# FFT-style convolution on one core: second pixels held behind the third weight chunk, and weight, transform and plane operations of the two-tile phase put in another order

## The chip, the core and the metric

The kernel runs on one core of a Trainium2 chip. The core has five engines that run side by side and meet only through semaphores. TensorE (PE) multiplies matrices; PEld is its load of the stationary operand. VectorE (DVE) and ScalarE (ACT) do elementwise work and move results out of PSUM, the accumulator memory of eight banks. GpSimd (POOL) does slow elementwise work. SyncE (SP) issues transfers, which sixteen DMA engines carry out. The metric is the device time of one execution in microseconds (us); lower is better. Of the kernel before, three runs are shown: 271.89, 271.96 and 272.75 us, median 271.96.

## The reference

The input is one image of 224 x 224 pixels with 96 channels; the weights are 7 x 7 taps from 96 to 96 channels, all bf16. The reference multiplies spectra, which is a circular convolution:

```
Xf = rfft2(x, axes=(1, 2))                     # 1 x 224 x 113 x 96
Wf = rfft2(pad(w to 224 x 224), axes=(0, 1))
Yf = einsum('bhwi,hwio->bhwo', Xf, Wf)
y  = irfft2(Yf, s=(224, 224), axes=(1, 2)).astype(bfloat16)
```

## The kernel before, in words

The image's width is cut into seven tiles of 32 pixel columns (index t). In the height direction the kernel uses blocks of 28 output rows and a short transform of them into 17 frequency slots (index s, 0 to 16); slots 0 and 16 are real, the others have three parts (real, imaginary and the difference of the two). Along the width the seven taps stay a direct convolution, in a form for two output pixels at a time that shares products.

The work of a tile has these steps.

1. **Transform** (`f_jobs`, `a_jobs`): matmuls of pixels with the transform matrix `Fm`; the result is moved ("evicted") from a PSUM bank into `xf`. For the first three tiles it is done in three parts of slots (`SH2`: 0-7, 8-12, 13-16). `jg` is the half of the image's rows; each half has its own pixel buffer.
2. **Planes** (`jit`): for a group of two or three slots VectorE forms `J` from `xf` in three operations: first four planes of differences of pixels, then one sum of parts, and third two planes made from the first four. Three `J` buffers take turns.
3. **Rounds** (`b_round`): one round is one slot of one tile. TensorE multiplies `xf` and `J` with the transformed weights `WF` into two banks. ScalarE makes a scaled copy (`tt_`), VectorE forms `u` from the first bank (which frees it) and `v` from the second. POOL then adds `v` and `u` into `yf` (`ysum`). Real slots have a single VectorE operation instead.
4. **Way back**: `yf` goes to a scratch array in DRAM, is read again with another layout (`tt`), multiplied with `G` and written out.

The weights are loaded in five chunks of columns (`wcut`), each as two transfers, and transformed on TensorE from `wq` (`prep_jobs`), in six groups of slots (`PGRP`). Group 0 comes before the rounds; the others are paced inside them. A group of the others has 12 matmul jobs and, on VectorE, three differences.

The order is written out by hand. Each engine runs its instructions in program order. `fills` is called twice in a round, as `mid` between the two banks and as `end`; it hands out jobs that `add(a, b, jobs)` has spread evenly over the call numbers a to b - 1. The eviction of a bank goes to VectorE or ScalarE by a running cost count (`evac`). Bank number n + 8 of the sequence waits for the eviction of bank n.

In the two-tile phase the rounds of tile 0 and tile 1 run together, tile 1 four rounds behind (`LAG`). `bursts` says in which round which group of planes is formed; a round's planes stand behind its `v`, and POOL's sum of that round waits for the last of them. Ahead of it lie the loads, set-up work on POOL, VectorE and ScalarE, the transform of tile 0's first half, filler matmuls on `wu` (`warm`) that compute nothing that is used, the transform of weight group 0, and the transform of the second half's first part. The first tile's pixels (`load_x(0, 0)`, `load_x(0, 1)`) are loaded into the tail of `WF`, which a late weight group overwrites; the second tile's loads wait for an eviction.

Of the kernel before, what the change touches and what calls it, by code (L numbers as in the profile page):

```python
# [17 lines left out]
NS = L // 2  # L18
# [14 lines left out]
PGRP = ((0, 2), (2, 5), (5, 8), (8, 11), (11, 14), (14, 17))  # L33
# [6 lines left out]
JGB = ((0, 3), (3, 6), (6, 9), (9, 12), (12, 15), (15, 17))  # L40
LAG = 4
# [3 lines left out]
NP2 = 0  # L45
WARM = 36
NWC = 5
BIAS = 3000.0


# [5 lines left out]
def kernel(  # L56
# [7 lines left out]
    _, H, W, C = x.shape  # L64
# [8 lines left out]
    C2 = C // 2  # L73
    assert NJ == 8
    SYNC = mybir.DependencyInfo(mybir.DependencyClass.Sync, mybir.DependencyReason.DATA)
# [57 lines left out]
    def dma(out_ap, in_ap):  # L133
        return DE.dma_start(out=out_ap, in_=in_ap)
# [18 lines left out]
    wqx = wtmp.tile([128, C - 1 + 127 * C + 1], BF16, name="wq")  # L153
# [20 lines left out]
    def load_x(t, jg):  # L174
        return load_rows(xbuf(t, jg), jg, t * 2 * TW, 2 * TW)

    wsrc = w.rearrange("kh kw i o -> (kh kw) (i o)")
    for jg in range(2):
        load_rows(xh_bufs[jg], jg, W - PAD, PAD)
    load_x(0, 0)  # L180
    wcut = [WC * c // NWC // 128 * 128 for c in range(NWC)] + [WC]
    for c0, c1 in zip(wcut, wcut[1:]):
        for k, n in ((PW - 1, 1), (0, PW - 1)):
            dma(wqx[2 * k:2 * (k + n), c0:c1],
                bass.AP(wsrc.tensor, wsrc.offset + k * C * C + c0, [[C * C, n], [C2, 2], [1, c1 - c0]]))
    load_x(0, 1)

    wu = cpool.tile([128, 128], BF16, name="wu")
    wur = wu[:].unsqueeze(1).to_broadcast([128, 4, 128])
# [2 lines left out]
    def warm(n):  # L192
        pwu = bank()
        for _ in range(n):
            TE.matmul(pwu[:].rearrange("p (a b) -> p a b", a=4), lhsT=wu[:, 0:128], rhs=wur, start=True, stop=True)
# [297 lines left out]
    def b_round(t, s, mid, end, ydve=False, planes=()):  # L493
# [26 lines left out]
        if s in REAL:  # L520
            for part in range(2):
                conv(b0, part * C, 0, part)
            SE.copy(out=tt_[:, 0:2 * C], in_=b0[:, 0:2 * C])
            mid()
            for mi, m in enumerate((2, 1)):
                for part in range(2):
                    conv(b1, (mi * 2 + part) * C, m, part)
            VE.tensor_tensor(out=yv.rearrange("p r m o -> p m r o"),
                             in0=tt_[:, 0:2 * C].rearrange("p (r o) -> p r o", o=C).unsqueeze(1).to_broadcast([128, 2, 2, C]),
                             in1=b1[:, 0:4 * C].rearrange("p (m r o) -> p m r o", m=2, r=2), op=ALU.add)  # L530
            load["a"] += 110 + 0.9 * 192
            load["v"] += 540
            for f in planes:
                f()
            end()
        else:
            v = tv_pool.tile([128, 2, 2, C], F32, name="v")
            if merge:
                conv(b0, 2 * C, 0, 0, both=True)
                conv(b0, 2 * C, 2, 0, add=True)  # L540
                conv(b0, 3 * C, 1, 0, add=True)
                conv(b0, 0, 0, 1)
                conv(b0, C, 0, 2)
                SE.mul(out=tt_[:], in_=b0[:, 0:4 * C], mul=-0.5)
                u, pr = tt_[:, 2 * C:4 * C].rearrange("p (m o) -> p m o", m=2), tt_[:, 0:2 * C]
            else:
                for part in range(3):
                    conv(b0, part * C, 0, part)
                conv(b0, 3 * C, 2, 0)
                conv(b0, 4 * C, 1, 0)  # L550
                u = tv_pool.tile([128, 2, C], F32, name="u")
                SE.mul(out=tt_[:, 0:3 * C], in_=b0[:, 0:3 * C], mul=-0.5)
                pr = tt_[:, C:3 * C]
            if puts:
                puts.pop(0)()
            if not merge:
                VE.scalar_tensor_tensor(out=u[:], in0=b0[:, 3 * C:5 * C].rearrange("p (m o) -> p m o", m=2), scalar=-0.5,
                                        in1=tt_[:, 0:C].unsqueeze(1).to_broadcast([128, 2, C]), op0=ALU.mult, op1=ALU.add)
            mid()
            for mi, m in enumerate((2, 1)):  # L560
                for pi, part in enumerate((1, 2)):
                    conv(b1, (mi * 2 + pi) * C, m, part)
            VE.scalar_tensor_tensor(out=v.rearrange("p m r o -> p m (r o)"),
                                    in0=pr.unsqueeze(1).to_broadcast([128, 2, 2 * C]), scalar=-2.0,
                                    in1=b1[:, 0:4 * C].rearrange("p (m q) -> p m q", m=2), op0=ALU.mult, op1=ALU.add)
            def ysum(eng):
                return eng.tensor_tensor(out=yv.rearrange("p r m o -> p m r o"), in0=v[:],
                                         in1=u.unsqueeze(2).to_broadcast([128, 2, 2, C]), op=ALU.add)
            if ydve:
                ysum(VE)  # L570
            last = None
            for f in planes:
                last = f()
            if not ydve:
                y = ysum(GE)
                if last is not None:
                    tc.add_manual_dep(y.ins, last.ins.name, SYNC, reason="sum after planes")
            load["a"] += 490 if merge else 410
            load["v"] += (560 if ydve else 250 if t < 2 else 0) + (560 if merge else 900)
            end()  # L580
# [119 lines left out]
    fj = [f_jobs(0, p) for p in range(3)]  # L700
    for p in range(3):
        for f in fj[p][0]:
            f()
    for _ in range(3):
        warm(9)
    for f in prep_jobs(0):
        f()
    last = [f() for f in fj[0][1]]
# [29 lines left out]
    def add(a, b, jobs):  # L738
        qs.append([a, b, jobs, len(jobs)])

    for gi in range(1, len(PGRP)):
        add(2 * PGRP[gi - 1][0], 2 * PGRP[gi - 1][1] - 1, prep_jobs(gi))
    for t in range(2):
        scr_tiles[t] = dr_pool.tile([TW, NJ, NS, 4 * C], BF16, name="scr")
    bursts = {}
    for g in range(len(JGB)):
        g0 = JGB[g][0]
        if g:
            bursts[(g0 - 2, 1 if g0 - 2 >= LAG else 0)] = (0, g)
        r1 = LAG + g0 - (3 if g == len(JGB) - 1 else 1)  # L750
        bursts[(r1, 0 if r1 < NS else 1)] = (1, g)
    bursts[(NS + LAG - 2, 1)] = (2, 0)
    nburst = len(bursts)
    for r in range(NS + LAG):
        if r == 0:
            add(0, 4, fj[1][1] + fj[2][1])
        for p in range(3):
            if r == (1, 3, 5)[p]:
                new_xf(1, SH2[p], SH2[p + 1])
                fj = f_jobs(1, p)  # L760
                if p == 2:
                    for jg in range(2):
                        fj[jg][-1] = then_load(fj[jg][-1], 2, jg)
                add(2 * r + 1, 2 * r + (5, 5, 4)[p], fj[0] + fj[1])
        for p in range(3):
            if r == SH2[p + 1] + 1 - (p == 2):
                new_xf(2, SH2[p], SH2[p + 1])
                fj = f_jobs(2, p)
                if p == 2:
                    for jg in range(2):  # L770
                        fj[jg][-1] = then_load(fj[jg][-1], 3, jg)
                add(2 * r, 2 * r + (8, 7, 5)[p], fj[0] + fj[1])
        if r == PGRP[-2][1] + 1:
            assert not any(q[2] for q in qs[:len(PGRP) - 1])
            wtmp_cm.__exit__(None, None, None)
            t_pool = ctx.enter_context(tc.tile_pool(name="tt", bufs=NTT, side="right"))
            t2_pool = ctx.enter_context(tc.tile_pool(name="tt2", bufs=1, side="right"))
            yo_pool = ctx.enter_context(tc.tile_pool(name="yo", bufs=2, side="right"))
            g_pool = ctx.enter_context(tc.tile_pool(name="gp", bufs=1, side="right"))
            GA = g_pool.tile([KA, 4 * B], BF16, name="GA")  # L780
            GB = g_pool.tile([128, 2, 4 * B], BF16, name="GB")
            GE.memset(GA[:], 0.0)
            GE.memset(GB[:], 0.0)
        if r == NS + 3:
            queue_c(0)
        for t in range(2):
            s = r - LAG * t
            if not 0 <= s < NS:
                continue
            now = bursts.pop((r, t), ())  # L790
            now = jit(*now) if now else ()
            both = LAG <= r < NS
            b_round(t, s, fills(qs, 2 * r + (t if both else 0)), fills(qs, 2 * r + (t if both else 1)), False, now)
    assert not bursts and nburst == 2 * len(JGB)
    if NP2:
        ps0_cm.__exit__(None, None, None)
        ps_cms = [tc.tile_pool(name="ps", bufs=NP2, space=bass.MemoryType.PSUM),
# [4 lines left out]
    for t in range(2, NT):  # L802
# [22 lines left out]
        for s in range(NS):  # L825
            now = ()
            if s in plan:
                g = plan[s]
                now = jit(t, g + 1) if g + 1 < len(JGB) else jit(t + 1, 0)
# [34 lines left out]
    for i, (g, q) in enumerate(order):  # L864
# [3 lines left out]
        k = i + 8 - LF  # L868
# [37 lines left out]
```

## Time and profile before

| | |
|---|---|
| median of the runs shown | 271.96 us |
| profiled execution, its own time | 272.2 us |
| its span | 270.5 us |
| TensorE busy | 258.7 us (96%) |
| VectorE busy | 213.9 us (79%) |
| ScalarE busy | 195.6 us (72%) |
| POOL busy | 95.6 us (35%) |
| granted TensorE clock | 1.00 |
| DMA, mean rate | 173 GB/s |
| chain that ended last | 74% TensorE |

The views give times in us from the start of the span. A timeline row has start, duration, engine, source line, operation, output and inputs, and in brackets how long the engine had been idle and what ended that. A duration of a merged row runs from the first start to the last end. All operations go through one recording helper, so that nearly every row has its line, L88; tiles tell the rows apart. A row by stretches has the stretch, its length, and the busy time of PE, PEld, DVE, ACT and POOL with the number of instructions in brackets, then the granted clock, the share of the DMA engines' time and GB/s. DMA rows of SPq show the issue, not the transfer.

### The profile page before, as it was taken

To read this page: it belongs to the slowest core of one execution; us is meant where nothing else is said; L and a number is where in the kernel's file an instruction comes from. 1 tells how busy PE (TensorE), PEld (TensorE's weight loads), DVE (VectorE), ACT (ScalarE), POOL (GpSimd) and SP (SyncE) were. 2 spreads that over 40 slices of the span, in tenths; PEclk is the share of its full clock that TensorE was granted. 3 is DMA by queue.
4 is the path that set the end of the run, shared out by engine and by line. 5 is a ranking of instruction groups with operands and counts; after the bars stand their busy time and mean duration, and the time that the engine had idled before them with its cause. 6 is when DMAs were issued, how large, how long until landed. Compare 5 with 4: busy or idle time off the path is not lost.

```text
span 270.5 us, 12170 instructions
## 1 busy us (share of the span) xinstructions
PE 258.7 (96%) x5149; PEld 237.8 (88%) x5149; DVE 213.9 (79%) x457; ACT 195.6 (72%) x483; POOL 95.6 (35%) x156
## 2 busy tenths in 40 slices
PE   8899998999999999999999999999999999899983
PEld 3679898999999989999999999998998989789862
DVE  5647999898889888779787888787898889778623
ACT  5549997568875657988988889887887865477113
POOL 7781032435536624431422222223222242422100
PEclk9999999999999999999999999999999999999999
DMA  6947010731121498986977477989649834887766
GB/s 168 232 124 200 23 47 2 204 105 49 43 77 63 126 276 157 292 247 177 298 206 217 116 205 244 251 210 349 222 125 163 269 103 147 200 235 203 221 118 202
DMA packets 47014, 46.78 MB, mean 173 GB/s; under 512 B 35286, under 2 KB 37986, under 8 KB 46960
## 3 DMA queue, kind: packets, MB, share of 16 engines
q1 hardware_dynamic: 44672, 43.94, 58.7%
q10 hardware_dynamic: 2288, 2.06, 2.7%
q8 instruction: 40, 0.66, 1.1%
q14 instruction: 14, 0.11, 0.2%
HBM read 24.65 MB, written 21.33 MB: 170 GB/s over the span
## 4 chain that ended last, share of the span: by engine, by line
PE 74%; DVE 7%; DMA 7%; ACT 5%; issue 3%; POOL 2%; SPq 1%; DVEq 0%; POOLq 0%; ACTq 0%
PE pb L88 74%; DMA tt<-scr 4%; ACT WF L88 3%; POOL ct L88 2%; DMA xf<-scrb 2%; DVE J L88 2%; DVE v L88 1%; DVE WF L88 1%; DVE u L88 1%; ACT xf L88 1%; DMA scrb<-yf 1%; SPq L88 1%; DVE yf L88 1%; DVE xf L88 1%; DVE wq L88 1%
## 5 line engine op out<-in xcount | busy, mean ns | idle before, releaser
L88 PE MATMUL pb<-WF,J 96*128 96x96 bf16 x2821 | 162.5, 206 | 1.1 <-DVE J L88 0.6
L88 PEld LDWEIGHTS <-J 96*128 96x128 bf16 x2821 | 138.1, 98 | 10.4 <-issue 2.6
L88 POOL TENSOR_TENSOR yf<-v,u 128x384 bf16<-128x384 f32 x79 | 78.6, 1008 | 151.7 <-issue 88.6
L88 ACT CAST xf<-pb 96x408 bf16<-96x408 f32 (+3 forms) x144 | 67.3, 486 | 8.1 <-PE pb L88 6.2
L88 PE MATMUL pb<-WF,xf 96*128 96x96 bf16 x952 | 60.2, 206 | 0.8 <-ACT xf L88 0.5
L88 DVE TENSOR_TENSOR J<-xf 96x1824 bf16<-96x1824 bf16 (+1 forms) x84 | 57.6, 724 | 0.1
L88 PEld LDWEIGHTS <-xf 96*128 96x128 bf16 x952 | 47.1, 98 | 1.2 <-ACT xf L88 0.6
L88 PE MATMUL pb<-Fm,xn 118*128 118x136 bf16 (+3 forms) x640 | 45.5, 199 | 0.9 <-DVE u L88 0.8
L88 PE MATMUL pb<-tt,Gm 102*84 102x384 bf16 (+1 forms) x132 | 32.7, 327 | 1.7 <-DMA tt<-scr 1.7
L88 ACT CAST WF<-pb 96x480 bf16<-96x480 f32 (+1 forms) x59 | 29.0, 570 | 5.7 <-PE pb L88 5.7
L88 PEld LDWEIGHTS <-xn 118*128 118x128 bf16 x640 | 30.4, 97 | 1.1 <-issue 1.1
L88 ACT CAST J<-pb 84x384 bf16<-84x384 f32 (+1 forms) x64 | 27.6, 488 | 2.4 <-PE pb L88 2.3
L88 ACT CAST yo<-pb 84x384 bf16<-84x384 f32 (+1 forms) x64 | 27.2, 482 | 1.9 <-PE pb L88 1.1
L88 DVE TENSOR_TENSOR J<-J 96x912 bf16<-96x912 bf16 (+2 forms) x42 | 22.8, 542 | 0.0
L88 PE MATMUL pb<-wq 98*128 98x120 bf16 (+1 forms) x288 | 21.3, 225 | 0.0
L88 PEld LDWEIGHTS <-wq 98*128 98x128 bf16 x288 | 19.5, 149 | 0.2
L88 PE MATMUL pb<-wu 128*128 128x512 bf16 (+1 forms) x80 | 17.6, 381 | 1.0 <-DVE ct L88 1.0
L88 PEld LDWEIGHTS <-wu 128*128 128x128 bf16 (+1 forms) x80 | 9.3, 118 | 8.2 <-issue 2.4
L88 DVE TENSOR_TENSOR yf<-v,u 128x384 bf16<-128x384 f32 x26 | 14.7, 566 | 0.9
L88 PEld LDWEIGHTS <-Gm 102*84 102x84 bf16 (+1 forms) x132 | 11.0, 117 | 2.7 <-DMA tt<-scr 2.1
L88 DVE CAST WF<-pb 96x480 bf16<-96x480 f32 (+1 forms) x13 | 7.5, 610 | 5.4 <-PE pb L88 5.3
L88 ACT COPY xf<-xf 96x816 bf16<-96x816 bf16 (+3 forms) x20 | 11.2, 618 | 0.0
(386 smaller groups left out, 233.4 us busy)
## 6 DMA issues: line engine op xcount, KB each, us to landing
scr<-yf SPq DMA_DIRECT2D x30, 288.0 KB
xn<-in_x_dram SPq DMA_DIRECT2D x12, 672.0 KB
tt<-scr SPq DMA_DIRECT2D x24, 336.0 KB
out_dram<-yo SPq DMA_DIRECT2D x12, 252.0 KB
out_dram<-J SPq DMA_DIRECT2D x12, 252.0 KB
tt<-scr SPq DMA_DIRECT2D x6, 288.0 KB
WF<-in_x_dram SPq DMA_DIRECT2D x2, 672.0 KB
out_dram<-tt SPq DMA_DIRECT2D x8, 168.0 KB
```

The lines of the kernel that those rows point to most:

```text
L88: r = fn(*a, **k)
```

## The change

1. The two transfers of the first tile's second pixels, `load_x(0, 1)`, are issued only when the second transfer of weight chunk 2, the third chunk, has landed (`HOLD`). They stand last among the first loads, as before.
2. The last filler ahead of weight group 0 is two banks of 11 matmuls instead of three of 9.
3. Weight group 1 is spread over fill calls 0 and 1 instead of 0 to 2.
4. The first tile's second part (second half) goes to fill calls 1 to 4 and its third part to calls 5 to 8; both were in calls 0 to 3.
5. Of the planes of a burst the first two stay where they were. The third is kept back (`rest`) and stands behind the `v` of the next round. POOL's sum waits for a round's planes only if there is more than one, so it no longer waits for a third plane that stands alone.
6. Tile 2's first planes are formed one round earlier.

In the two-tile phase the cost count then sends some evictions to the other engine; later, one output eviction goes to VectorE instead of ScalarE. Counts of matmuls are otherwise the same.

```
+HOLD = 2
...
+    wdma = []
     for c0, c1 in zip(wcut, wcut[1:]):
         for k, n in ((PW - 1, 1), (0, PW - 1)):
-            dma(wqx[2 * k:2 * (k + n), c0:c1],
-                bass.AP(wsrc.tensor, wsrc.offset + k * C * C + c0, [[C * C, n], [C2, 2], [1, c1 - c0]]))
-    load_x(0, 1)
+            wdma.append(dma(wqx[2 * k:2 * (k + n), c0:c1],
+                bass.AP(wsrc.tensor, wsrc.offset + k * C * C + c0, [[C * C, n], [C2, 2], [1, c1 - c0]])))
+    for d in load_x(0, 1):
+        tc.add_manual_dep(d.ins, wdma[2 * HOLD + 1].ins.name, SYNC, reason="second pixels behind the weights")
...
                 y = ysum(GE)
-                if last is not None:
+                if len(planes) > 1:
                     tc.add_manual_dep(y.ins, last.ins.name, SYNC, reason="sum after planes")
...
-    for _ in range(3):
-        warm(9)
+    for n in (11, 11):
+        warm(n)
...
-        add(2 * PGRP[gi - 1][0], 2 * PGRP[gi - 1][1] - 1, prep_jobs(gi))
+        add(2 * PGRP[gi - 1][0], 2 * PGRP[gi - 1][1] - (2 if gi == 1 else 1), prep_jobs(gi))
...
+    rest = []
...
-    bursts[(NS + LAG - 2, 1)] = (2, 0)
+    bursts[(NS + LAG - 3, 1)] = (2, 0)
...
-            add(0, 4, fj[1][1] + fj[2][1])
+            add(1, 5, fj[1][1])
+            add(5, 9, fj[2][1])
...
-            now = jit(*now) if now else ()
+            now = jit(*now) if now else []
+            now, rest = rest + now[:2], now[2:]
...
-    assert not bursts and nburst == 2 * len(JGB)
+    assert not rest and not bursts and nburst == 2 * len(JGB)
```

## The prediction

> **What bounds the kernel now.** I read the page's engine table first, then the chain, then the tensor engine's own timeline for every wait it shows, then what stood behind each wait.
>
> ```profile
> PE 258.7 (96%) x5149; PEld 237.8 (88%) x5149; DVE 213.9 (79%) x457; ACT 195.6 (72%) x483; POOL 95.6 (35%) x156
> ```
>
> TensorE is busy for 258.7 of 270.5 us, and the chain of waits is 74% TensorE. So an edit can gain only by taking work off TensorE or by closing one of its few gaps. The gaps that the change can reach are in the first 100 us (timeline by start, duration, engine; brackets: idle before, and what ended it):
>
> ```profile
> 10.96 5.99 PE L88 MATMUL pb<-wu 128*128 128x512 bf16 x27
> ...
> 16.57 3.20 PEld L88 LDWEIGHTS <-wq 98*128 98x128 bf16 x48
> ...
> 29.20 0.33 PE L88 MATMUL pb<-WF,J 96*128 96x96 bf16 x4 [0.36 <-DVE WF L88]
> ...
> 29.89 0.33 PE L88 MATMUL pb<-WF,xf 96*128 96x96 bf16 x4 [0.19 <-DVE WF L88]
> ...
> 45.71 0.95 PE L88 MATMUL pb<-Fm,xn 118*128 118x32 bf16 x32 [0.80 <-DVE u L88]
> ...
> 97.70 0.47 PE L88 MATMUL pb<-WF,J 96*128 96x96 bf16 x7 [0.62 <-DVE J L88]
> ```
>
> The reader should see four things: 27 filler matmuls on `wu` that compute nothing; the weight transform (`wq`) starting straight behind them without a wait; 0.55 us of waiting for weight differences at 29; and 0.80 and 0.62 us of waiting for VectorE at 45.7 and 97.7. Between them TensorE runs without a break.
>
> VectorE by stretches (columns: stretch, length, then busy time of PE, PEld, DVE, ACT, POOL):
>
> ```profile
> 20.00:25.00 5.00, 4.54 (x106) 4.42 (x103) 4.60 (x9) 4.66 (x12) 1.07 (x3) 1.00 0.68 175
> 25.00:30.00 5.00, 4.45 (x121) 4.24 (x120) 3.35 (x7) 4.95 (x12) 0.00 (x0) 1.00 0.48 123
> 30.00:35.00 5.00, 5.00 (x114) 5.00 (x113) 5.00 (x10) 4.44 (x12) 1.29 (x2) 1.00 0.02 5
> 35.00:40.00 5.00, 5.00 (x140) 5.00 (x138) 5.00 (x11) 4.98 (x14) 1.33 (x2) 1.00 0.17 62
> 40.00:45.00 5.00, 4.80 (x104) 4.58 (x102) 5.00 (x8) 3.43 (x11) 1.39 (x2) 1.00 0.01 3
> ```
>
> VectorE has 1.65 us to spare from 25 to 30 and nothing from 30 to 45. There it is a second bound, and the 0.80 us wait is its backlog. From 60 to 100 it is busy for 33.8 of 40 us (sums of the same view).
>
> **The hold and the filler: -1.08 us.** The 27 fillers take 16.78 - 10.96 = 5.82 us from start to start, 0.216 each; five fewer are 1.08 us, if the weights have landed by 16.57 - 1.08 = 15.49. How far the loads are is told by the loads behind them: in the built program each of SP's loads waits for the one eight places ahead of it.
>
> ```profile
> 9.16 0.57 SPq L88 DMA_DIRECT2D wq<-in_w_dram  x1
> ...
> 9.77 0.59 SPq L88 DMA_DIRECT2D WF<-in_x_dram  x1
> ...
> 10.93 0.27 SPq L88 DMA_DIRECT2D WF<-in_x_dram  x1
> ```
>
> The load at 9.16 waited for weight chunk 1, the one at 10.93 for chunk 2: landed by about 9.1 and 10.9, 1.8 apart, so chunk 3 at about 12.6 (estimate). The load at 9.77 is the big part of the first tile's second pixels, 0.69 MB. It now goes out at 12.6 instead of 9.77, behind the third chunk.
>
> ```profile
> 12.00:13.00 1.00, 1.00 (x6) 0.49 (x5) 0.10 (x1) 0.00 (x0) 0.74 (x4) 1.00 1.16 261
> 13.00:14.00 1.00, 1.00 (x7) 0.41 (x5) 0.00 (x0) 0.00 (x0) 0.72 (x4) 1.00 1.08 248
> 14.00:15.00 1.00, 1.00 (x6) 0.47 (x5) 0.00 (x0) 0.00 (x0) 0.71 (x5) 1.00 1.04 275
> 15.00:16.00 1.00, 1.00 (x7) 0.47 (x5) 0.00 (x0) 0.00 (x0) 0.77 (x5) 1.00 0.97 246
> 16.00:17.00 1.00, 1.00 (x9) 0.57 (x8) 0.00 (x0) 0.00 (x0) 0.92 (x4) 1.00 0.46 123
> 17.00:18.00 1.00, 1.00 (x20) 1.00 (x19) 0.78 (x2) 0.54 (x2) 0.88 (x2) 1.00 0.12 49
> ```
>
> The last column is GB/s. From 12.6 on about 1.04 MB are still to move, whatever their order. With the 0.72 MB of pixels last, the weights are through about 2.9 us before the loads' end near 17, at about 14 (bounds: 13.7 if the pixels never shared with them, 15.3 if they share as now). Either way that is before 15.49, so the 1.08 us is taken whole. The pixels then land at 12.6 + 4.2 = 16.8, or 18.0 if the queue runs dry for 1.2 us (from the first issue at 0.8 to the first bytes near 2.0). Their transform starts at 19.73 - 1.08 = 18.65: covered by 0.65 to 1.9 us. If that cover were gone, TensorE would wait one for one. On SP nothing but the second tile's loads stands behind the held ones; they wait for an eviction at 20.77 anyway and move up 1.08. Their first use falls earlier too, by 1.08 + 0.55 + 0.4 (16 fewer 32-column matmuls ahead of it), at about 26.2. The queue shows 0.48 share from 25 to 30, so its first half should be in by 25 to 26: covered, barely.
>
> **Weights and transforms in the two-tile phase.** The second weight group (12 jobs, 3 differences) is now all in round 0; the first tile's remaining six transform jobs go to rounds 0 to 3. The count of matmuls and evictions is the same. By the built order the three differences now stand before round 1's u on VectorE, at about 25.2 to 27.0, for a use at about 27: the 0.55 us goes.
>
> Then VectorE's backlog. From the end of the first planes (23.06 + 0.46 = 23.52) to the end of the u that frees the bank (45.32 + 0.34 = 45.66) are 22.14 us; 0.21 and 1.61 of them idle, so 20.3 of work. The new order adds one 512-element eviction there (0.68) and puts one third plane (0.62) behind that u: 20.4. VectorE starts 1.08 earlier, at 22.44. Without idling the u would end at 42.8, 2.8 earlier. I add 0.25 for ScalarE's last weight eviction ahead of the differences and 0.5 for its scaled copy of round 3 (its queue of nine weight evictions at 0.46 and what follows runs to 33.5; VectorE is there at 33.0). So TensorE gets that bank 2.0 us earlier. That includes the 1.08 and the 0.55: of the ideal 1.08 + 0.55 + 0.80 = 2.43, 2.0 is had and about 0.4 comes back as smaller waits in rounds 3 to 6, the first where the third plane is needed one round after its pair (about 31.6). Bounds: 1.1 (only the filler) to 2.43.
>
> **The planes.** J(2,0) goes one round up: its first plane ends near 95.7 instead of 97.65, for a use near 97.1, so the 0.62 goes; I take 0.6. What is late next is round 18's u behind it, with no reader waiting on TensorE.
>
> Twelve third planes now follow the next round's v, and POOL's sum of that round no longer waits for them. No row shows a third plane beside a sum. The nearest are the first two planes:
>
> ```profile
> 42.90 1.95 DVE L88 TENSOR_TENSOR J<-xf 96x1824 bf16<-96x1824 bf16 x2
> ...
> 50.58 1.40 DVE L88 TENSOR_TENSOR J<-xf 96x1824 bf16<-96x1824 bf16 x2
> ...
> 88.43 2.62 POOL L88 TENSOR_TENSOR yf<-v,u 128x384 bf16<-128x384 f32 x2 [1.60 <-issue]
> ...
> 60.76 0.36 DVE L88 SCALAR_TENSOR_TENSOR u<-pb,tt__1662 128x192 f32<-128x192 f32 x1 [0.46 <-POOL yf L88]
> ```
>
> Beside a sum at 42.59 the pair took 1.95 instead of 1.40: 0.55 dearer. At 88.43 two sums took 2.62 instead of 2 x 1.00, beside a plane. So an overlap costs one side about 0.6. From below: sums that now end 0.6 to 2 us sooner end the 0.46 waits like the one at 60.76. Bounds per burst: -0.46 to +0.55 on VectorE; on TensorE nothing as long as VectorE has slack. I take 0.2 in all.
>
> The Trainium skill (SBUF — State Buffer, "Who interferes with whom" and the list ahead of it) calls this an exclusive lock: whichever starts first keeps the pair and the other blocks. By that rule the plane, next in VectorE's own queue, would start first and the sum would wait 0.6: the sum would be -2.6 instead of -2.4. The 2.62 row agrees; the 1.95 row is the other order.
>
> **Sum.** -2.0 at 45.7, -0.6 at 97.7, +0.2 for overlaps: -2.4 us. Behind 98 TensorE runs to 178 in one piece and the later waits for stored sums move along; one output eviction changes from ScalarE to VectorE (about 0.5 against 0.48), priced at nothing because both have over 10% idle from 180 to 220 (busy 33.5 and 32.5 of 40). The profiled execution took 272.2 us, span 270.5; so 269.8 for it. It stands 0.24 above the median of the runs, 271.96, so for the median I say 269.6.
>
> **Rivals.**
> - Only the filler pays, and VectorE's backlog stays: its rounds 3 to 6 stall as much as now, because each third plane costs it 0.55. For it: 5.00 of 5.00 busy from 30 to 45. Against: 1.65 idle just ahead that the new order fills. -1.08 to -1.3: 270.8. Chance 0.16.
> - The weights are not there at 15.5, so the filler turns into a wait and only the gaps close. For it: no row shows the fifth chunk's landing, only that it is before 16.57. Against: 1.04 MB at 250 GB/s with the pixels last. -1.3: 270.6. Chance 0.06.
> - Slower: the sum takes the shared path first, and each of the twelve third planes waits for most of it. Place: VectorE between v and the next u, in the rounds behind each burst. Price 0.55 for the 1.00 sum by the 1.95 row, twelve times 6.6 us. With 2.6 gained elsewhere it decides from (2.6 + 0.8) / 0.55, about six planes that TensorE feels in full, and gives 276 at most; I put it at 273. Against: 16% of VectorE's time from 60 to 100 is idle. Chance 0.08.
> - The held pixels land after 18.65, at up to 1.5 lost: 269.6 + 1.5 = 271.1, on the edge of no change. Chance 0.06.
>
> The forecast has 0.64.
>
> **How the numbers follow.** No change means within 0.3%, 0.8 us, about what a measurement can tell here. Faster is the forecast, the first two rivals and some of the last, less their share above 271.1: 0.80; same 0.12; slower 0.08. The range: from 268.6 (every gap closes and some waits of u go too: 3.05 + 0.3) up to 271.2, leaving the slower case and part of the late-pixel case out. The forecast's own range is 268.8 to 270.3.
>
> **What will show it.** 22 fillers with `wq` right behind, without a wait, at about 15.7; pixels' transform at 18.65 without a wait; no wait for WF differences near 27; the wait for u at 43 to 44 under 0.4; no wait for J near 95; third planes near 0.62 or near 1.2, sums near 1.0 or near 1.6. I am wrong if `wq` or the second pixels wait, or if TensorE shows new waits for u or J from 30 to 95.

## The result and the profile after

The changed kernel takes 270.03 us (median; 269.54 to 274.14), the kernel before, measured beside it, 272.21. The ratio is 0.991, with a 95% interval from 0.9887 to 0.9934: 2.4 us faster, between 1.8 and 3.1. Ratios here and below leave disturbed executions out and medians do not, so the two can differ by some tenths of a per cent. The profiled execution of the changed kernel took 270.74 us, 0.7 above its own median; its span is 269.0.

The engine table of the page after the change:

```profile
PE 257.9 (96%) x5144; PEld 237.1 (88%) x5144; DVE 214.3 (80%) x457; ACT 195.5 (73%) x483; POOL 99.4 (37%) x156
```

TensorE's work fell by 0.8 us (258.7 before: the five fillers), VectorE's grew by 0.4, and POOL's grew by 3.8 although it does the same operations. TensorE's timeline, the rows that answer to those shown before, the waits in the first 100 us that are new, and the mark T that is used below:

```profile
10.98 4.91 PE L89 MATMUL pb<-wu 128*128 128x512 bf16 x22
...
16.21 3.15 PE L89 MATMUL pb<-wq 98*128 98x100 bf16 x48 [0.32 <-DMA wq<-in_w_dram]
...
27.22 0.34 PE L89 MATMUL pb<-WF,J 96*128 96x96 bf16 x4
...
43.60 0.95 PE L89 MATMUL pb<-Fm,xn 118*128 118x32 bf16 x32 [0.21 <-DVE u L89]
...
58.42 0.47 PE L89 MATMUL pb<-WF,J 96*128 96x96 bf16 x7 [0.49 <-DVE J L89]
...
87.43 0.47 PE L89 MATMUL pb<-WF,J 96*128 96x96 bf16 x7 [0.37 <-DVE J L89]
...
98.63 0.52 PE L89 MATMUL pb<-Fm,xn 118*128 118x136 bf16 x6
```

The weights' transform waits 0.32 for its last chunk, so it starts 0.57 earlier than before (16.78), not 1.08. The wait for weight differences near 28 is gone. The wait for `u` fell from 0.80 to 0.21 and its row comes 2.11 earlier (45.71 before). The wait for `J` at 97.7 is gone. Two waits for `J` are new, 0.49 and 0.37, both for a third plane. (A wait of 0.46 for `xf` near 21, which the prediction's "without a break" passes over, is there before and after alike.) The last row, the first 136-column matmuls of the third tile, is the end of the stretch that the change touches; before they started at 100.52. So the lead there is 1.89 us.

VectorE in four of the stretches shown before (length, busy time of PE, PEld, VectorE, ScalarE, POOL, then clock, DMA share and GB/s):

```profile
25.00:30.00 5.00, 5.00 (x138) 5.00 (x135) 4.87 (x11) 5.00 (x14) 0.15 (x1) 1.00 0.33 92
30.00:35.00 5.00, 5.00 (x122) 5.00 (x119) 4.56 (x9) 4.81 (x13) 2.23 (x2) 1.00 0.17 64
35.00:40.00 5.00, 5.00 (x146) 5.00 (x144) 5.00 (x10) 4.51 (x13) 1.00 (x1) 1.00 0.02 3
40.00:45.00 5.00, 4.79 (x121) 4.67 (x120) 5.00 (x11) 4.13 (x11) 2.08 (x2) 1.00 0.01 3
```

From 25 to 30 VectorE is now busy for 4.87 of 5.00 (3.35 before) and has 0.44 to spare from 30 to 35: the hole was filled, and the backlog behind it is smaller.

Third planes and sums on one timeline, in two rounds:

```profile
31.51 0.62 DVE L89 TENSOR_TENSOR J<-J 96x912 bf16<-96x912 bf16 x1
31.67 1.35 POOL L89 TENSOR_TENSOR yf<-v,u 128x384 bf16<-128x384 f32 x1 [0.80 <-DVE v L89]
...
56.87 3.34 POOL L89 TENSOR_TENSOR yf<-v,u 128x384 bf16<-128x384 f32 x3 [1.40 <-issue]
56.93 0.53 DVE L89 SCALAR_TENSOR_TENSOR v<-tt__1594,pb 128x384 f32<-128x384 f32 x1
57.39 0.97 DVE L89 TENSOR_TENSOR J<-J 96x912 bf16<-96x912 bf16 x1
```

Where the plane starts first it keeps its 0.62 and the sum takes 1.35 instead of 1.00. Where a sum is already running (from 56.87, three in a row), the plane takes 0.97. Three of the nine large third planes (96x912) up to 100 us take 0.97 to 0.99 (at 57.39, 70.02, 86.40); the other six keep 0.62 to 0.64. The first and the third of them are the ones that TensorE waits for.

Behind 100 us one wait differs from before by much:

```profile
203.79 0.52 PE L89 MATMUL pb<-tt,Gm 102*84 102x384 bf16 x2 [1.10 <-DMA tt<-scr]
```

Before it was 0.38, at 204.80. In a second profiled execution of the same kernel the wait is 0.16. The lead over the kernel before falls here by 0.7, as much as the profiled execution lies above its median; that the one makes the other is not shown.

### The profile page after: what moved, and what is told of

Its sections match the earlier page's. It is cut to its first block, busy times and chain, and to the rows that moved or that the text cites. A ratio compares the mean times of both kernels' runs of the same rounds, so it can differ in the third digit from the quotient of the medians.

```text
span 269.0 us, 12171 instructions
## 1 busy us (share of the span) xinstructions
PE 257.9 (96%) x5144; PEld 237.1 (88%) x5144; DVE 214.3 (80%) x457; ACT 195.5 (73%) x483; POOL 99.4 (37%) x156
## 4 chain that ended last, share of the span: by engine, by line
PE 64%; DMA 12%; DVE 11%; ACT 7%; issue 3%; SPq 2%; DVEq 0%; ACTq 0%
PE pb L89 64%; DMA tt<-scr 5%; DMA wq<-in_w_dram 5%; DVE J L89 4%; ACT WF L89 3%; ACT xf L89 2%; DVE v L89 2%; DVE WF L89 2%; SPq L89 2%; DMA xf<-scrb 2%; DVE u L89 1%; DMA scrb<-yf 1%; DVE yf L89 1%; DVE xf L89 0%; DVE tt L89 0%
## 5 line engine op out<-in xcount | busy, mean ns | idle before, releaser
L89 POOL TENSOR_TENSOR yf<-v,u 128x384 bf16<-128x384 f32 x79 | 81.4, 1042 | 147.3 <-issue 86.9
L89 DVE TENSOR_TENSOR J<-xf 96x1824 bf16<-96x1824 bf16 (+1 forms) x84 | 56.9, 716 | 0.1
L89 DVE TENSOR_TENSOR J<-J 96x912 bf16<-96x912 bf16 (+2 forms) x42 | 24.2, 576 | 0.0
L89 PE MATMUL pb<-wu 128*128 128x512 bf16 (+1 forms) x75 | 16.5, 382 | 1.1 <-DVE ct L89 1.1
```

The costliest lines, as they stand in the source:

```text
L89: r = fn(*a, **k)
```

## The experiments

The runs were made in three groups, each with the kernel before beside it. Its medians there were 272.54, 272.43 and 272.54 us; beside the first row of the changed kernel it was 272.21. Edits are shown against the changed kernel. W is the start of the weights' transform, T the start of the third tile's first 136-column matmuls, both read from the one profiled execution of each kernel; T - W is what TensorE needs for the 1920 matmuls between them, the same number in every kernel, waits included.

| kernel | W | T | T - W | median | ratio to before, 95% interval |
|---|---|---|---|---|---|
| before | 16.78 | 100.52 | 83.74 | | |
| changed, first | 16.21 | 98.63 | 82.42 | 270.03 | 0.991 [0.9887, 0.9934] |
| changed, again | 15.90 | 98.30 | 82.40 | 270.12 | 0.9909 [0.9876, 0.9943] |
| loads and filler only | 15.72 | 99.82 | 84.10 | 272.53 | 0.9992 [0.9963, 1.0021] |
| order only | 16.80 | 99.88 | 83.08 | 271.83 | 0.9972 [0.9942, 1.0001] |
| planes only | 16.80 | 100.38 | 83.58 | 272.47 | 0.9983 [0.9954, 1.0012] |
| order undone | 15.70 | 99.59 | 83.89 | 271.49 | 0.9967 [0.9945, 0.9988] |
| filler of 27 | 16.81 | 99.14 | 82.33 | 270.73 | 0.9944 [0.9924, 0.9964] |
| no hold | 16.46 | 98.88 | 82.42 | 270.08 | 0.9917 [0.9898, 0.9936] |
| hold to the fifth chunk | 15.71 | 101.66 | 85.95 | 273.57 | 0.9996 [0.9968, 1.0024] |
| tile 2's planes late | 15.76 | 99.64 | 83.88 | 272.76 | 1.001 [0.9985, 1.0034] |
| sum waits again | 15.93 | 99.06 | 83.13 | 270.61 | 0.9937 [0.9919, 0.9956] |
| third plane before `v` | 15.88 | 100.77 | 84.89 | 273.45 | 1.004 [1.0023, 1.0057] |
| two bursts keep the third plane | 16.49 | 97.69 | 81.20 | 268.73 | 0.9872 [0.9851, 0.9893] |

### The changed kernel again

No edit.

> The changed kernel again, beside its parts on the same chip. Expected -2.2 us against the kernel before (ratio 0.992), with the lead built up by 45 us and partly lost to DMA waits behind 200 us. If the lead of 1.9 us that the first profile shows at 100 us is what counts, a profile in which the wait for the stored sums near 204 us stays at 0.4 us should end about 0.7 us sooner.

T - W is 82.40 against 82.42: the places and sizes of the waits up to 100 us repeat (0.22 for `u`, 0.49 and 0.36 for `J`). W moves by 0.3 between executions and T with it, so the lead at T is 1.9 to 2.2. Here the weights wait for nothing: the 22 fillers take 5.09 us instead of 4.91. The trace gives this execution a granted clock of 0.948 over the whole, so nothing behind T is read from it but the wait at 202.82; what was expected of its end stays untested.

### The loads and the filler alone

```
-            add(1, 5, fj[1][1])
-            add(5, 9, fj[2][1])
+            add(0, 4, fj[1][1] + fj[2][1])
...
-    bursts[(NS + LAG - 3, 1)] = (2, 0)
+    bursts[(NS + LAG - 2, 1)] = (2, 0)
...
-            now, rest = rest + now[:2], now[2:]
```

and group 1's spread and the rule of the sum as in the kernel before.

> The kernel before with the hold of the second pixels and 22 fillers alone. Theory A (each edit pays by itself what its stage showed): the weight transform starts at about 16.2 instead of 16.8, -0.5 to -0.6 us in all, ratio 0.998. Rival B (VectorE's backlog from 30 to 45 is the real bound, so an earlier start is only waited off there): the wait for u at 45 grows by as much, ratio 1.000.

TensorE's timeline:

```profile
15.72 3.15 PE L89 MATMUL pb<-wq 98*128 98x100 bf16 x48
...
28.47 0.33 PE L89 MATMUL pb<-WF,J 96*128 96x96 bf16 x4 [0.67 <-DVE WF L89]
...
45.00 0.95 PE L89 MATMUL pb<-Fm,xn 118*128 118x32 bf16 x32 [0.80 <-DVE u L89]
...
97.00 0.94 PE L89 MATMUL pb<-WF,J 96*128 96x96 bf16 x18 [0.62 <-DVE J L89]
...
103.62 0.30 PE L89 MATMUL pb<-WF,xf 96*128 96x96 bf16 x3 [0.41 <-issue]
```

Here the start is 1.06 earlier, without a wait. But T - W is 0.36 longer than before: the wait for weight differences grew from 0.36 to 0.67, and 0.80 and 0.62 stay. A lead of 0.70 is left at T. At 103.62, in the middle of a group of eight matmuls, TensorE idles 0.41 more, for which the view names no releaser; behind it the lead is 0.1, and the time shows no gain (0.9992). Neither theory holds as told: the start came earlier, but the wait for `u` did not take it back. Alone, this part buys nothing that can be measured.

### The order alone

```
-HOLD = 2
...
-    for n in (11, 11):
-        warm(n)
+    for _ in range(3):
+        warm(9)
...
-    bursts[(NS + LAG - 3, 1)] = (2, 0)
+    bursts[(NS + LAG - 2, 1)] = (2, 0)
...
-            now, rest = rest + now[:2], now[2:]
```

with the hold taken out, and the rule of the sum as in the kernel before.

> The kernel before with the second weight group in round 0 and the first tile's remaining transforms spread to rounds 0 to 3, nothing else. Theory A: the 0.55 us of waits for weight differences near 29 go and the 0.80 us wait for u at 45.7 shrinks because VectorE fills its 1.6 us of idling from 25 to 28: -0.9 to -1.3 us, ratio 0.996. Rival B (the work on VectorE is only moved and the backlog stays): the 0.55 comes back in the wait for u, ratio 1.000.

The 0.55 for weight differences is gone, 0.80 at 45.09 and 0.62 at 97.06 stay: a lead of 0.64 at T, 0.7 us in the time (0.9972, the interval just reaches no change). The first half of theory A holds, the second does not: filling VectorE's hole at 25 to 30 does not by itself shorten the wait for `u`.

### The planes alone

```
-HOLD = 2
...
-    for n in (11, 11):
-        warm(n)
+    for _ in range(3):
+        warm(9)
...
-            add(1, 5, fj[1][1])
-            add(5, 9, fj[2][1])
+            add(0, 4, fj[1][1] + fj[2][1])
```

with the hold taken out, and group 1's spread as in the kernel before.

> The kernel before with the third planes behind the next round's v, the sum not waiting for a third plane alone, and tile 2's first planes one round earlier. Theory A: the wait for u at 45.7 falls by about 0.6 and the 0.62 at 97.7 goes, against new waits for third planes of 0.9 us as in the first profile: -0.3 us, ratio 0.999. Rival B (the planes are the whole gain): -1.5 us or more, ratio 0.994. Rival C (third planes beside POOL's sums cost VectorE 0.35 each and TensorE feels it): slower, ratio 1.002 or more.

The 0.80 for `u` and the 0.62 for tile 2's planes are gone, but at another price (VectorE's third plane, then TensorE's waits):

```profile
34.06 0.63 DVE L88 TENSOR_TENSOR J<-J 96x912 bf16<-96x912 bf16 x1
...
34.75 0.47 PE L88 MATMUL pb<-WF,J 96*128 96x96 bf16 x7 [0.62 <-DVE J L88]
...
60.16 0.47 PE L88 MATMUL pb<-WF,J 96*128 96x96 bf16 x7 [0.49 <-DVE J L88]
```

The third plane behind the next `v` is late at 34.75 already, as my step 3 had feared ("the first where the third plane is needed one round after its pair (about 31.6)"). A third wait, 0.37 at 89.17, is that of 87.43 in the changed kernel. In the whole change the wait near 34 is not there: VectorE gets to that plane 2.5 us earlier (31.51 against 34.06), TensorE to the weights only 0.6. This comes nearest to theory A. The three parts alone give 0.70 + 0.64 + 0.14 = 1.48 at T, together 1.9 to 2.2. My reading is that each removes a delay that the others would otherwise wait behind; the next run tests it.

### The order undone

```
-        add(2 * PGRP[gi - 1][0], 2 * PGRP[gi - 1][1] - (2 if gi == 1 else 1), prep_jobs(gi))
+        add(2 * PGRP[gi - 1][0], 2 * PGRP[gi - 1][1] - 1, prep_jobs(gi))
...
-            add(1, 5, fj[1][1])
-            add(5, 9, fj[2][1])
+            add(0, 4, fj[1][1] + fj[2][1])
```

> The changed kernel with the old spread of weight group 1 and of the first tile's transform jobs. Alone, these two moves brought the mark near 100 forward by .64, the loads .70 and the planes .14, together 1.9 to 2.2: about .5 belongs to the three acting together. If that part hangs on VectorE being filled where it idled (25 to 30), undoing the order costs its own .64 and the .5: waits for WF differences near 28 (.5 to .7) and for J near 34 (.3 to .6) are back, mark 99.5 to 99.8, time 1.0 to 1.2 above the changed kernel. Rival: the common part lies between loads and planes alone, and undoing the order costs .64: mark 98.9 to 99.3, no wait near 34, time .5 to .7 above.

```profile
28.46 0.33 PE L89 MATMUL pb<-WF,J 96*128 96x96 bf16 x4 [0.72 <-DVE WF L89]
...
33.95 0.47 PE L89 MATMUL pb<-WF,J 96*128 96x96 bf16 x7 [0.60 <-DVE J L89]
```

Both waits came back on TensorE's timeline, T at 99.59 as expected, the time 271.49: 1.4 above the changed kernel, where the order alone had been worth 0.7. So the common part does hang on the order, which fills the hole at 25 to 30.

### The old filler

```
-    for n in (11, 11):
-        warm(n)
+    for _ in range(3):
+        warm(9)
```

> The changed kernel with the old filler of 3 x 9 matmuls. My step 1 as the trace corrected it: the weights' transform starts at 16.8 again instead of 15.7 to 16.2, the mark near 100 comes .4 to 1.0 later (99.0 to 99.6), and the time is .4 to 1.0 above the changed kernel. Rival: VectorE is the bound behind the start and takes the later start from its own waits, so that the mark moves under .2 and the time not at all.

W is 16.81, T - W 82.33, as in the changed kernel: the start goes through to T one for one, 0.5 to 0.8 later than in the two executions of the changed kernel, and the time is 0.6 to 0.7 higher, though the intervals of the two ratios overlap. By T the VectorE rival falls.

### No hold

```
-    for d in load_x(0, 1):
-        tc.add_manual_dep(d.ins, wdma[2 * HOLD + 1].ins.name, SYNC, reason="second pixels behind the weights")
+    load_x(0, 1)
```

> The changed kernel without the hold: the second pixels go out at about 9.8 again, beside the last weight chunks, and the filler stays at 22. With pixels behind the fifth chunk the weights had landed by 15.0, behind the third chunk at 15.7 to 16.1. My theory, sharing delays the last chunk: it lands at 16.2 to 16.8, the weights' transform waits .5 to 1.1 and the mark near 100 comes .3 to .8 later; the time .3 to .8 above the changed kernel. Rival: the landing does not hang on the pixels, the transform starts at 15.7 to 16.1 as with the hold, and mark and time are the changed kernel's within .2.

```profile
16.46 3.11 PE L88 MATMUL pb<-wq 98*128 98x100 bf16 x48 [0.57 <-DMA wq<-in_w_dram]
```

TensorE's row for the weights' transform: it waits 0.57, against 0.32 and 0 with the hold. So the hold brings the weights' transform forward by 0.25 to 0.56 (16.46 against 16.21 and 15.90), and T follows by 0.25 to 0.58. Five more kernels of the table have the same start, with this hold and a filler of 22 from 10.96 to 10.98 on; their W lies between 15.70 and 15.93. (Where two bursts keep their third plane, W is 16.49 for another reason: there the filler starts at 11.75, behind a wait for the first pixels.) The kernel without a hold was profiled once. In the time none of it is seen: 270.08 against 270.03 and 270.12. The gain of step 1 comes from the filler; what the hold adds is at the edge of what can be told here.

### The hold moved to the last chunk

```
-HOLD = 2
+HOLD = 4
```

> The changed kernel, but the second pixels go out only behind the fifth and last weight chunk. The weights then share the queue with no pixels at all. If the pixels behind the third chunk held up the last chunks (bound of my step 1: 13.7 without sharing), the weights' transform starts without a wait at about 15.7 and the last chunk lands before 15; the pixels then go out at 14 to 15 and land at about 18 to 19, about as the transform needs them: time unchanged within .5. Rival: the loads are bound by something else than the sharing, and the last chunk lands at 15.5 to 16.1 all the same. Then the pixels go out at 16, land near 19.5 to 20, and TensorE waits for them .5 to 1 us: time .5 to 1 us above the changed kernel.

TensorE's rows, then SyncE's issue of the pixels, then stretches with the granted clock (third last column) and GB/s (last):

```profile
15.71 3.15 PE L89 MATMUL pb<-wq 98*128 98x100 bf16 x48
20.38 1.87 PE L89 MATMUL pb<-Fm,WF 118*128 118x64 bf16 x32 [1.52 <-DMA WF<-in_x_dram]
```

```profile
15.01 0.69 SPq L89 DMA_DIRECT2D WF<-in_x_dram  x2
```

```profile
12.00:13.00 1.00, 1.00 (x6) 0.49 (x5) 0.10 (x1) 0.00 (x0) 0.74 (x4) 1.00 0.93 218
13.00:14.00 1.00, 1.00 (x7) 0.41 (x5) 0.00 (x0) 0.00 (x0) 0.72 (x5) 1.00 0.37 91
14.00:14.50 0.50, 0.50 (x4) 0.26 (x3) 0.00 (x0) 0.00 (x0) 0.35 (x3) 1.00 0.15 52
14.50:15.00 0.50, 0.50 (x4) 0.21 (x3) 0.00 (x0) 0.00 (x0) 0.35 (x3) 1.00 0.00 0
...
18.50:19.00 0.50, 0.36 (x6) 0.23 (x4) 0.50 (x2) 0.50 (x2) 0.36 (x2) 1.00 0.30 86
19.00:20.00 1.00, 0.00 (x0) 0.00 (x0) 0.47 (x1) 0.17 (x1) 0.84 (x3) 0.86 0.00 0
20.00:21.00 1.00, 0.62 (x13) 0.65 (x14) 0.00 (x0) 0.00 (x0) 0.71 (x2) 0.50 0.00 0
...
26.00:27.00 1.00, 1.00 (x20) 1.00 (x18) 0.65 (x1) 1.00 (x3) 0.00 (x0) 0.73 1.01 283
```

Without any pixels beside them the weights have landed by 15.01, where the pixels, which wait for them, go out; so sharing does cost the last chunk up to 1.2 (16.21 in the changed kernel's first execution), and about 1.5 without a hold (16.46). Most of the bytes were moved by 13.5. Some 50 KB trickle on until 14.5, and the release follows 0.5 later: 1.5 us from the end of the bulk to the release. The pixels then need 5.4 us from issue to the transform that waits for them (15.01 to 20.38), also in a queue that is empty when they go out; their traffic ends near 19, some 1.4 before the release. TensorE waits 1.52, and during that wait the granted clock falls to half, from about 19.7 to 26.5 (0.86 in its stretch is 0.28 of it at half, 0.73 is 0.54). T - W is 3.5 longer than in the changed kernel, over twice the wait. Executions with a mean clock of 0.987 took 273.5 to 273.8 us, two with 0.999 and 1.00 took 269.75 and 271.61; in between (0.990 to 0.994) they lie from 271.95 to 274.08. So the time goes with the clock, though not strictly. The rival came nearer for the time, my theory for the landing.

### Tile 2's first planes late

```
-    bursts[(NS + LAG - 3, 1)] = (2, 0)
+    bursts[(NS + LAG - 2, 1)] = (2, 0)
```

> The changed kernel, but tile 2's first planes are formed in the old round. My step 4 says: TensorE's wait of .62 for J near 95.5 to 96 is back, the mark near 100 comes .6 later (98.9 to 99.2), and the time rises by .6, to 270.6 or 270.7. Rival: VectorE has slack by then and its other work moves up, so that the wait is under .2 and the time unchanged.

```profile
96.24 0.94 PE L89 MATMUL pb<-WF,J 96*128 96x96 bf16 x18 [0.62 <-DVE J L89]
97.93 1.24 PE L89 MATMUL pb<-WF,J 96*128 96x96 bf16 x25 [0.41 <-DVE J L89]
...
103.51 0.30 PE L89 MATMUL pb<-WF,xf 96*128 96x96 bf16 x3 [0.48 <-issue]
```

```profile
96.55 0.99 POOL L89 TENSOR_TENSOR yf<-v,u 128x384 bf16<-128x384 f32 x1 [2.33 <-DVE J L89]
96.80 1.07 DVE L89 TENSOR_TENSOR J<-J 96x608 bf16<-96x608 bf16 x1
```

The 0.62 is back on TensorE's timeline, and 0.41 beside it. The second wait is for the third plane, which in this place starts beside a running sum and takes 1.07 (in the kernel before, in the old round but with its pair, 0.46). So part of what is lost comes of the old round and the split of the planes together. T - W is 1.46 longer than in the changed kernel, more than the 0.6 of my step 4. Of its lead over the kernel before it loses 0.7 more right behind T (the changed kernel 0.15). All of that lies in the row at 103.51, and it has its like at 103.62 in the kernel with the loads alone. What ended those two waits the view does not name. The median is 2.6 to 2.7 above the changed kernel's. Five executions, the profiled one among them, took 271.5 to 271.6 us, about 1.5 above it, and for these the marks account. Six took 272.4 to 274.7, and why these were slower was not settled.

### The sum waits for a lone third plane again

```
-                if len(planes) > 1:
+                if last is not None:
```

> The changed kernel, but POOL's sum of a round waits again for the last plane that stands with that round, a lone third plane too. My theory: beside a running sum the third plane takes .97 to .99 us instead of .62, and that lateness is what TensorE's new waits for J at 58.4 (.49) and 87.4 (.37) are made of. Then the third planes are all near .62, the two waits fall to about .14 and 0, and the first 136-column matmuls of the third tile come at about 97.9 to 98.2 instead of 98.3 to 98.6. But the sums end later, and u's waits for POOL (.43 to .46 before) may come back on VectorE. Time: 0.3 to 0.7 us below the changed kernel. Rival: the waits come from the place of the third plane behind the next v, and the lock costs the path nothing. Then they stay within .1 of .49 and .37, and the time is the changed kernel's within 0.3 us.

Planes, sums and the wait on one timeline:

```profile
57.03 1.00 POOL L89 TENSOR_TENSOR yf<-v,u 128x384 bf16<-128x384 f32 x1 [1.40 <-issue]
57.56 0.97 DVE L89 TENSOR_TENSOR J<-J 96x912 bf16<-96x912 bf16 x1
...
58.58 0.47 PE L89 MATMUL pb<-WF,J 96*128 96x96 bf16 x7 [0.70 <-DVE J L89]
...
59.66 0.36 DVE L89 SCALAR_TENSOR_TENSOR u<-pb,tt__1719 128x192 f32<-128x192 f32 x1 [0.41 <-POOL yf L89]
```

My expectation falls, and so does that of the rival. The plane still takes 0.97, because the sum beside it is that of the round before, which this edit does not hold. And `u` waits for POOL again (0.41, 0.46, 0.40), as before the change. The waits for `J` become 0.70, 0.29 and 0.41, T - W grows by 0.7 and the median by 0.5, where the intervals overlap. So the dropped wait of the sum is worth 0.7 us by T, 0.5 to 0.7 in all. That is the gain that step 5 had told of in "sums that now end 0.6 to 2 us sooner end the 0.46 waits".

### A lone third plane in front of `v`

```
+            if len(planes) == 1:
+                planes.pop()()
             VE.scalar_tensor_tensor(out=v.rearrange("p m r o -> p m (r o)"),
```

> The changed kernel, but a third plane that stands alone goes in front of its round's v instead of behind it. It is then never beside that round's sum and is ready about .55 us earlier plus the .35 that the lock cost. My theory: third planes at .62, the waits for J at 58.4 and 87.4 are gone, mark near 100 about .8 earlier, time about 269.3 (.8 below the changed kernel). Rival: v frees a PSUM bank .62 later, and TensorE waits for v or the u behind it instead: mark and time unchanged or up to .6 later.

```profile
57.28 0.99 POOL L89 TENSOR_TENSOR yf<-v,u 128x384 bf16<-128x384 f32 x1 [1.40 <-issue]
57.34 1.42 DVE L89 TENSOR_TENSOR J<-J 96x912 bf16<-96x912 bf16 x1
...
58.82 0.47 PE L89 MATMUL pb<-WF,J 96*128 96x96 bf16 x7 [0.93 <-DVE J L89]
```

Both theories were too kind. In front of `v` the plane starts 0.05 to 0.11 behind the sum of the round before and takes 1.38 to 1.44, six times up to 100 us. In every such row it ends about 0.49 after the sum: here 57.28 + 0.99 = 58.27, and 57.34 + 1.42 = 58.76. It hardly runs until the sum is through. TensorE's waits for `J` are 0.93, 0.47 and 0.87, T is 2.1 later than in the changed kernel, the time 273.45, slower than before.

### Two bursts keep their third plane

The pairs at 55.04 and 84.35 in the changed kernel belong to rounds 7 (tile 1) and 15 (tile 0). Their third planes are the two that TensorE waits for.

```
-            now, rest = rest + now[:2], now[2:]
+            cut = 3 if (r, t) in ((7, 1), (15, 0)) else 2
+            now, rest = rest + now[:cut], now[cut:]
```

> The changed kernel, but the two bursts whose third plane came late to TensorE (58.4 and 87.4) keep it with the first two, so that it stands ahead of the next u instead of behind the next v, and that round's sum waits for it. My theory: what those waits are made of is the place behind v (and with it a sum that is already running). Then both third planes are near .62, the waits of .49 and .37 are gone, the third tile's first 136-column matmuls come at 97.5 to 97.8, and the time is .6 to .8 below the changed kernel. Rival: the u behind the plane then frees its bank .62 late and its sum is late too, so TensorE waits for u, or VectorE for POOL, as much as was gained: mark 98.3 to 98.7, time unchanged within .3.

```profile
56.87 0.62 DVE L89 TENSOR_TENSOR J<-J 96x912 bf16<-96x912 bf16 x1
57.41 0.34 DVE L89 SCALAR_TENSOR_TENSOR u<-pb,tt__1595 128x192 f32<-128x192 f32 x1
57.62 2.96 POOL L89 TENSOR_TENSOR yf<-v,u 128x384 bf16<-128x384 f32 x3 [1.95 <-issue]
...
58.67 0.36 DVE L89 SCALAR_TENSOR_TENSOR u<-pb,tt__1656 128x192 f32<-128x192 f32 x1 [0.46 <-POOL yf L89]
```

The plane takes 0.62, ahead of the held sum. Both waits for `J` are gone, and no other took their place on TensorE: from 22 to 100 us its only listed wait is 0.15 for `u`. Two `u` wait for POOL, 0.46 here and 1.14 at 91.57, and TensorE shows no wait for either. T - W is 81.20, 1.2 shorter than in the changed kernel. The time is 268.73, ratio 0.9872 with an interval from 0.9851 to 0.9893: clearly faster than the kernel before, and 1.3 us below the changed kernel, more than the 0.6 to 0.8 expected. Against the changed kernel, measured in another group, the intervals of the ratios just touch; T - W is the stronger sign.

## Why the prediction was right, and which terms were not

The forecast was 269.6 us, 2.4 below the kernel before; measured were 270.03 and a ratio that gives 2.4 again. The traces show less, a lead of 1.9 to 2.2 at T, so that the exact agreement of the time is in part luck. "Only the filler pays" falls with the filler alone (no gain), the late pixels with the changed kernel's trace (no wait). At T the sum can be checked by parts. Predicted: 1.08 from the start and 1.32 behind it. Measured in the two executions of the changed kernel: 0.57 and 0.88 from the start, and 83.74 - 82.42 = 1.32 behind it. The second figure agrees by a balance of errors. Up to the row near 44 the lead grows by 1.54 behind the start (2.11 - 0.57), where 0.92 was told (2.0 - 1.08). At the two waits for third planes it falls from 2.09 to 1.43 and from 1.63 to 1.09, 1.20 in all, where 0.2 was told. At tile 2's planes it grows by 0.78, where 0.6 was told. Some 0.2 come back in between. The listed waits understate this: a wait of 0.49 took 0.66 off the lead, one of 0.37 took 0.54, and the 0.62 that went gave the 0.78, each 0.16 to 0.17 more than its bracket.

**The filler (step 1): right mechanism, the landing mis-sized.** Start gained: 0.57 and 0.88 instead of 1.08 (the whole 1.08 in one other kernel with the hold). The term that failed is "the weights are through about 2.9 us before the loads' end near 17, at about 14": it took the end of the bulk of the traffic for the landing. The run with the hold at the fifth chunk has 1.5 us between the two, 1.0 of trickle and 0.5 from the last bytes to the release. The landing times that I had read off the waiting loads contain that time; from 12.6, two more chunks at the same spacing of 1.8 give 16.2, and 15.7 or less (where W shows no wait) to 16.2 was measured. The bound for sharing, 15.3, fails in the same way (16.46 without a hold). Of the rival "the weights are not there at 15.5" a part came true in one execution, a wait of 0.32 that took the place of filler.

**The second pixels (step 1): right, but the cover was thinner than told.** The transform starts at 19.20 without a wait. The landing told, 16.8 to 18.0, was early too. By the 5.4 us from issue to release, pixels issued at 12.92 are there at 18.3 at the earliest (estimate), 0.9 before their use. Moved two chunks further back they cost 3 us, twice what the rival of late pixels allowed; the clock at half behind the wait is the likely rest.

**Weight differences (step 2): right.** The 0.55 went, alone and in the whole.

**VectorE's backlog (step 3): right mechanism, the size by luck.** Predicted 2.0 at the row near 44, measured 2.11 and 2.41. But the 2.0 held 1.08 for the start, of which 0.57 and 0.88 came; behind the start it was 1.5 instead of 0.9. The 0.4 that should come back in rounds 3 to 6 did not show as waits; the planes alone show where it would have been (0.62 at 34.75).

**Tile 2's planes (step 4): right, and worth a little more than the 0.6 taken:** 0.78 in the lead. When undone in the changed kernel it is 1.03 in two waits and 1.46 in T - W, because there the third plane meets a sum as well.

**The third planes (step 5): mis-sized.** I took "0.2 in all" because "on TensorE nothing as long as VectorE has slack". TensorE waits 0.49 and 0.37 for two of them: 0.86, and their repair was worth 1.2 to T. VectorE did have slack from 60 to 100 (33.97 of 40 busy); what matters is not its slack, but when one plane is ready for one reader. Behind the next `v` it is ready 0.5 us later, and 0.35 later still beside a sum. Three planes started early enough in a running sum to be dearer. The gain on the other side, `u` no longer waiting for POOL, was real and 0.5 to 0.7.

The Trainium skill (SBUF — State Buffer, "Who interferes with whom") lets the first to start keep the shared pair and blocks the other. The trace agrees on who is slowed: with the plane first the sum takes 1.35, with the sum first the plane takes 0.97 to 1.44, the later the sum's end the more. It disagrees a little on the amount: from the plane's start to the sum's end lie 0.93 in the row at 57.34, and the plane is 0.80 dearer. By the rule I had put the plane first throughout. Six of the nine large planes keep their 0.62 to 0.64, two of them in the last 0.15 us of a sum; the other three start in the middle of a sum of the round before. The sum of -2.6 by the rule was no nearer than the -2.4 by the rows.

**The slower rival** had the right mechanism and put it at every plane: a price of 0.55 each, 273 us. With the plane in front of `v` it costs 0.8 for each of six and the time is 273.45. Behind `v` it takes hold of three planes only.

**Behind 98 us** 0.15 of the lead is lost up to 117 in the profiled execution of the changed kernel (1.89 to 1.74) and none from there to 195; no cause was shown. The waits for stored sums near 203 are 0.38 before, and 1.10 and 0.16 in the two executions: they differ between two executions of one kernel by 0.94.

## What to carry to other kernels

When a load's landing is the term, count from a release that the trace shows to the next release, not to the end of the bulk of the traffic: here 1.5 us lie between. Before an operation is moved behind another, look up its one reader and what is running on the engine that shares a path with it at the new place; idle time of the engine as a whole does not cover it. And undo single places, not the whole move: keeping two of the moved planes where they were brought 1.2 us more by T.

## What the runs showed of the hardware that was not expected

- In a wait of 1.52 us on TensorE its granted clock fell to half, from about 0.9 us after its last matmul ended (18.86, clock 0.86 in the stretch from 19 to 20) to about 26.5 (0.73 in the stretch from 26 to 27): some 6.8 us at half. The Trainium skill (TensorE: Matmul & The Clock Gate, "Part 1: The HAM clock gate") tells of a free-running activity window of some 3.4 us. The length agrees, two such windows; but the page lets the clock fall after at least one idle window, and here it fell after 0.9 us of idling. One profiled execution shows this.
- A third plane of 96x912 that starts in a running POOL sum ends 0.48 to 0.50 us after it, wherever in the sum it starts (0.05 to 0.9 behind the sum's start). Smaller ones end sooner: the plane of 96x608 at 96.80, beside the sum from 96.55 (tile 2's first planes late), 0.33 after it. In both cases that is about 0.13 less than the plane takes alone (0.62 and 0.46).
- A load's last bytes and its release lie apart: 0.5 us for the weights (hold at the fifth chunk: 52 GB/s from 14.0 to 14.5, 0 from 14.5 to 15.0, the next issue at 15.01), some 1.4 us for the pixels there (86 GB/s from 18.5 to 19, 0 from 19 on, release at 20.38).
